# Relu-squared attention followed by a GELU MLP on one core: the same operations in a new written-out order

## The chip, the core and the metric

The kernel runs on one core of a Trainium2 chip. Its time is device microseconds per execution. Several executions were timed, and one more was taken with the hardware profiler; that one gives the trace that this document reads. An engine's name in the profile stands for: PE (TensorE, matmuls), PEld (TensorE's weight loads, which overlap PE), DVE (VectorE), ACT (ScalarE), POOL (GpSimd, which here issues the loads), SP (SyncE, which issues stores and the transposing DMAs).

## What is computed

The reference, cut to its core: attention with a squared relu in place of the softmax, over 8 batches, 12 heads, 448 rows and 64 columns a head, then an MLP of 768 to 2048 to 768 with an exact GELU over the 3584 rows that result.

```python
scores = scale * np.matmul(q, k.transpose(0, 1, 3, 2))        # q, k, v: (8, 12, 448, 64)
attn = np.maximum(scores, 0.0) ** 2 / S
attn_out = np.matmul(attn, v)                                 # heads side by side -> x (3584, 768)
h = x @ w_in                                                  # (768, 2048)
g = 0.5 * h * (1.0 + erf(h * inv_sqrt2))
out = g @ w_out                                               # (2048, 768), float32
```

## The kernel before

**The work.** A batch's attention goes by three groups of four heads. For each group and each of seven key blocks of 64, TensorE makes scores (tile `ps`, line 806, four 64-row matmuls that run side by side), ScalarE or VectorE scales them and cuts them at zero into `a_sq` (lines 823 and 825), one of the two squares them (835 on VectorE, 833 on ScalarE), and after the seventh block TensorE multiplies with `v_sb` into `pav` (line 885), which is copied out as `xT` (550, 548). The MLP's two products are made by a scheme with seven products for eight (Strassen's kind): halves of operands are added or subtracted by VectorE (`t_x`, `ws`, `s_sb`, `t_sb`), TensorE multiplies (`pe`, line 1103; `pb`, line 1256; `pso`, line 1432), and VectorE or ScalarE gathers the parts (`part`, `osb`). GELU is on ScalarE. Output rows are stored from `osb` (three buffers) by SyncE, lines 1385 and 1393.

**The operands' way.** Batches 0 and 1 are transposed on TensorE (`tp`, lines 667 and 696). From batch 2 on, q and k are loaded by GpSimd (`nq`, `nk`, lines 506 and 588) and turned by transposing DMAs that SyncE issues (line 724, `kT<-nk` and `qT<-nq`). A batch's loads wait behind small copies on GpSimd (`gate`, lines 761 and 770) until the turns of the batch before have landed, because they fill the same tile; the last batch's v load stands behind such a copy too.

**What sets the order.** Every operation is an `Op` in one list. A table, `ORDER`, names all of them one after the other, with the engine that runs each: `P` and `Q` TensorE (`Q` takes two small PSUM banks in place of a wide one), `A` ScalarE, `D` VectorE, `G` GpSimd, `S` SyncE, `Z` a matmul on zeros whose result nothing reads. The number is the operation's place in the list. So `D46` in the table says that operation 46, which either engine could do, is done by VectorE. `place()` walks the table:

```python
for word in ORDER.split():
    if word[0] == "Z":
        op, eng = next(fills), "PE"
    else:
        op, eng = self.open[int(word[1:])], names[word[0]]
        if word[0] == "Q":
            op.split()
```

Each engine then runs its own operations strictly in the table's order, and waits by semaphores for what its next operation needs. A second table, `HOMES`, gives the buffer of each tile in the wide PSUM banks (`w`, 3), the small ones (`f`, 2) and the `a_sq` and `part` buffers (`a`, 14). Times in the planner that wrote the tables are not in the kernel.

The words that the prediction speaks of: `P102`, the product with v of batch 0, group 1, second half; `P270`, a product of the first MLP block (`pe`); `P1313`, the first product with v of batch 7; `G2`, the identity matrix for the transposes; `G3`, `G6`, k of batch 0, groups 1 and 2; `G1079`, v of batch 7; `S1099`, `S1119`, `S1118`, `S1291`, `S1098`, stores; `S1266` to `S1271`, the six turns of batch 7 (even: k; odd: q; two for each group); `S1068`, `S1069`, the last two turns of batch 6.

Of the kernel before, what the change touches and what calls it, by code (L numbers as in the profile page):

```python
# [99 lines left out]
A13 A19 D16 G2 Q17 D18 P20 D21 Q14 D15 G3 P22 D23 P42 A43 P45 D46 P39 A40 G4 P32 P24 P36 A37 D33 P96  # L100
Z672 A97 D25 P54 Z1024 A55 D41 D44 D47 G6 P26 D27 G7 Q28 D29 P57 A58 G10 P30 D31 P34 D35 D38 P51 A52
P72 D73 D59 D53 P69 A70 D71 D56 Q114 P60 A61 D62 A115 G5 P48 G121 A49 P66 A67 D68 G8 P87 A88 D50 G9
D74 Q78 A79 D116 P99 A100 P84 D85 P63 Q75 A64 A65 D76 D77 A80 P105 A106 D98 P93 P108 D94 A109 D107
G11 P144 A145 P134 D135 P111 A112 P81 A82 A83 G120 D101 P132 D133 G12 P146 A147 D89 D95 D86 P167
P179 A180 P161 A162 P148 D168 A149 G124 P136 D113 P90 A91 A92 P173 D137 D110 Q164 A165 D174 P102
A103 P117 D104 A118 A119 D169 D253 P176 A177 G125 P138 D139 D175 D163 D181 P170 A171 D178 D172 P245
A246 P185 P194 A186 D187 P200 A195 D196 A201 D166 P249 A250 G123 P150 A151 P191 P197 A198 P188 D189
A192 G129 P142 D143 G122 G128 P140 D141 D190 D199 D255 P203 A204 D205 P182 A202 P215 D216 D193 P209
A210 A183 A184 P251 A252 P247 A248 D254 P221 A222 P212 A213 G127 G126 P206 A207 Q224 A225 G131 P261
P278 D257 P268 D256 D258 D260 D279 D262 D226 D259 G152 A208 G153 Q227 P218 A223 A219 D220 P285 A269  # L110
A286 P264 P281 D265 D282 P263 P280 D211 A228 D229 A217 P273 D283 P270 P287 D271 D274 D288 G243 G130
A214 Q230 D266 P290 D291 A231 A232 D376 P276 A284 P293 A294 A277 A275 P378 P395 P380 P397 D374 D375
D377 D379 P381 D383 A292 A384 A267 D396 D400 P385 P402 A403 A386 P398 A382 A399 D412 D413 D415 P416
P433 A401 A417 A434 P390 P404 D405 A406 P407 D408 P419 A289 D391 D414 P387 P436 D388 P423 P440 A272
D458 A409 A420 G240 G241 S233 P410 P393 D450 D451 A437 P425 A424 P442 D426 A441 D443 A394 A389 A411
P428 S234 Q302 D459 A303 P314 A315 G155 G156 G158 G159 A427 P445 D446 A447 P431 P448 Q308 A309 D429
D453 D454 P317 A449 A318 P418 P435 D438 D421 D460 P462 D456 A432 A392 P464 D457 A422 A439 A463 D465
A444 P320 A321 P311 A312 D319 D452 P305 P466 A467 A306 A430 D455 D310 D304 P468 D469 S236 G239 G242
S235 P329 P341 A342 S238 A330 P335 A336 A307 D461 D313 P470 D471 D316 P472 S237 P368 D494 D322 D331
A369 P362 P338 A339 G154 G157 G160 G244 G295 G296 G297 P474 D475 D337 S477 P326 D495 D496 D473 P323  # L120
A363 D364 A327 D328 D340 A324 P344 A345 D346 P332 A333 A325 P498 A499 P500 P353 D501 D334 D343 S478
A354 D355 P359 P350 A351 A360 D497 D352 P502 D503 P365 A370 A366 P347 A348 A349 P356 D357 D367 A358
A361 P504 D505 P506 S479 P532 A533 P523 D524 D507 P526 A527 P508 G298 P520 D521 D522 P514 A515 G299
G300 P371 P517 A518 P529 A530 P510 D372 D373 D588 D586 D509 D587 D534 P590 P607 A608 A591 D589 P592
D595 D516 P597 P614 A615 D598 P610 P593 D624 A611 A594 P609 D612 P602 P619 A531 P616 A613 A519 D620
D617 A618 A621 D603 P626 P643 A596 D644 P599 D600 S482 S481 A627 S483 A601 P628 P645 D528 D648 A649
D631 A632 P629 A630 P605 P622 A606 D511 D625 D525 P633 P650 D634 A623 P646 P635 S480 P547 Q538 A651
P655 A539 S476 A548 D636 A637 P638 D647 D656 A657 P641 P652 D639 A640 P544 A545 G484 G487 P541 D653
D542 A642 G301 G490 Q535 A536 P556 A557 P574 P658 A659 A575 D678 D676 D677 P680 A681 D558 P553 D537
D554 D549 D540 D679 G485 G486 G488 G489 G491 G492 P565 A566 A546 P568 A569 S661 G666 P682 D683 P684  # L130
A555 D570 D543 A685 P562 A654 A563 P577 A578 A604 S512 S660 S662 P550 D551 D552 P686 P688 P725 P571
A572 A726 P559 P716 A717 D687 D564 D696 P690 D576 D689 A718 D560 D561 D573 D579 D691 D567 P719 D720
P728 A729 S663 G669 G493 P580 A581 A582 P692 D693 P700 P722 S695 S513 S665 G672 D697 G667 G668 P734
A723 D735 D721 D701 P583 A584 A585 P731 P749 D750 P702 D703 P752 A753 P740 D741 P704 A705 P792 A732
D698 P706 D699 P708 P809 D727 D724 P794 P811 D707 D733 D788 D789 D736 P799 P816 A730 A810 D709 P712
A751 D817 P821 D814 D791 D790 D713 A793 D797 P710 A798 P795 A815 D800 D711 P812 A813 P804 D822 A796
D805 P755 A823 Q737 A756 P743 A744 P818 D826 D827 P828 P845 A846 A757 P830 P847 D819 P824 D829 P831
D833 P801 D738 A739 D850 A851 P848 A849 A834 P835 P852 A853 D802 P807 A803 A808 D832 P837 A825 P854
A745 G670 G671 D878 D836 P840 D838 S864 D855 S862 S715 D742 S664 P782 A783 Q764 A765 P857 D858 A859
S863 P843 P860 A861 D880 D766 D841 D879 P882 S714 A844 A806 A856 P933 P773 S694 P746 D747 G673 D748  # L140
A774 A934 G674 S867 G868 P884 A883 D885 D754 A839 P758 P779 D759 D760 D775 P767 D881 P886 A887 A842
A780 A768 D781 D769 P888 D889 P890 D891 A820 D898 D900 P776 A777 A778 P761 A762 P930 P770 A771 D899
D784 A763 P892 A931 D893 P894 D772 P918 A919 D895 S865 G871 G675 G874 P948 D949 G869 G870 S897 P927
A928 D929 P902 P945 D946 P960 A961 P785 A786 S866 P924 A925 A926 D947 P954 D955 P904 D903 D901 D905
P936 A937 D920 D950 P921 P906 D907 G872 G873 G875 P908 D909 P910 A787 D992 D962 D911 D990 D932 P912
D913 A938 A935 P914 S916 S896 S1066 G876 A922 A923 S1067 S1065 S1068 D915 S917 P994 A995 P942 A943
Q966 P939 D967 P957 A958 Q951 P1011 G1070 D991 D993 P997 P1001 S1064 S1069 G1073 G877 G1076 A940
G1071 G1072 G1074 D941 D956 A998 P1018 A1002 A1019 P1003 D1004 P996 P1013 A1012 D999 D1016 A1005
A968 A1000 P1023 P1006 D1007 A1008 P1014 D1015 P1030 P1047 A1048 D1024 P1020 D1028 D1021 P1032 P1049
D1052 A1017 A1031 D1035 A1022 A1036 P1033 P1050 A1051 A1034 D959 D1029 P1009 P1037 P1054 D1055 P1039  # L150
P1056 D1038 D1040 P1026 D1057 P1042 P1059 D1043 D1080 D1060 D1081 A1041 A1027 A952 P1045 P1062 A1046
A1010 A1063 P1084 A1025 D953 P984 P969 A970 A971 A1053 P978 P1086 D1085 D1082 D944 P1088 D1087 P1090
D979 D985 A1044 A1089 A1061 P972 A973 P1138 D1139 A1058 D1091 P963 A964 P1135 D1136 P975 A976 A965
D1102 A974 A977 D986 P1094 D1095 P1092 D1093 D1083 P981 P1126 D1100 D1101 G1075 A982 D983 G1077
G1078 P1144 A1145 P1104 A1127 A980 P1096 D1097 S1099 P1153 D1154 P1159 A1160 D1128 P987 D988 D989
P1123 A1124 P1150 A1151 D1140 D1155 P1106 A1105 D1107 P1129 P1120 A1121 D1122 D1152 P1132 A1130
P1108 D1109 P1198 P1196 P1213 A1133 P1215 P1110 A1214 D1103 P1112 D1218 D1111 D1197 D1113 A1131
A1161 D1201 P1114 P1116 D1192 D1193 D1134 D1195 D1115 D1117 S1119 A1125 A1137 P1162 A1163 P1141
A1142 A1143 P1168 A1169 Q1147 P1199 A1148 D1194 P1216 D1217 A1202 P1203 P1220 A1221 P1156 A1157
A1158 Q1186 D1200 P1205 P1222 D1146 D1204 D1206 P1208 D1223 A1164 A1224 P1225 P1232 P1249 A1233  # L160
A1250 D1209 A1210 P1228 A1229 D1226 D1230 D1231 P1234 P1251 D1254 A1219 D1237 P1235 P1252 D1236
A1255 D1253 A1227 A1207 P1211 A1238 A1212 D1187 D1149 P1239 P1256 A1240 A1257 P1241 P1258 D1259
D1242 P1180 A1260 D1181 Q1174 A1243 A1175 P1261 P1244 D1262 A1263 P1247 P1264 D1245 A1265 A1248
# [1607 lines left out]
```

## Time and profile before

| what | value |
|---|---|
| median of 3 runs | 359.67 us (358.12 to 360.7) |
| the profiled execution's own time | 358.11 us |
| its span, first to last instruction | 356.3 us |
| granted TensorE clock | 1.0 throughout |
| PE busy | 348.5 us, 98% |
| PEld busy | 250.1 us, 70% |
| DVE busy | 306.0 us, 86% |
| ACT busy | 262.1 us, 74% |
| POOL busy | 102.9 us, 29% |
| DMA packets | 123465, 43.01 MB |

The span is the sum that a prediction works on; 1.8 us of the execution lie around it. Busy PE counts matmuls whose ends are modelled, so it says that matmuls follow each other without a gap, not that each runs at its peak.

### The profile page before, as it was taken

To read this page: it belongs to the slowest core of one execution; us is meant where nothing else is said; L and a number is where in the kernel's file an instruction comes from. 1 tells how busy PE (TensorE), PEld (TensorE's weight loads), DVE (VectorE), ACT (ScalarE), POOL (GpSimd) and SP (SyncE) were. 2 spreads that over 40 slices of the span, in tenths; PEclk is the share of its full clock that TensorE was granted. 3 is DMA by queue.
4 is the path that set the end of the run, shared out by engine and by line. 5 is a ranking of instruction groups with operands and counts; after the bars stand their busy time and mean duration, and the time that the engine had idled before them with its cause. 6 is when DMAs were issued, how large, how long until landed. Compare 5 with 4: busy or idle time off the path is not lost.

```text
span 356.3 us, 9246 instructions
## 1 busy us (share of the span) xinstructions
PE 348.5 (98%) x3853; PEld 250.1 (70%) x3853; DVE 306.0 (86%) x524; ACT 262.1 (74%) x431; POOL 102.9 (29%) x138
## 2 busy tenths in 40 slices
PE   7799999999999999999999999999999999999995
PEld 4577789855599555896557965669669856878663
DVE  3999999999898999789996998879987998769563
ACT  4999978999968995478985689879897896126100
POOL 8565842295183101603714129001000000000000
PEclk9999999999999999999999999999999999999999
DMA  9999999999999726999899979538009001012222
GB/s 174 198 204 203 186 192 176 163 158 161 170 154 179 114 44 116 102 199 118 114 166 137 188 101 122 74 107 139 2 2 182 30 2 46 2 45 90 88 90 88
DMA packets 123465, 43.01 MB, mean 121 GB/s; under 512 B 100896, under 2 KB 120096, under 8 KB 123424
## 3 DMA queue, kind: packets, MB, share of 16 engines
q0 software_dynamic: 84432, 22.47, 66.7%
q1 hardware_dynamic: 38448, 19.50, 26.1%
q8 instruction: 30, 0.49, 0.5%
q10 hardware_dynamic: 544, 0.46, 0.4%
q14 instruction: 11, 0.09, 0.1%
HBM read 45.61 MB, written 11.01 MB: 159 GB/s over the span
## 4 chain that ended last, share of the span: by engine, by line
PE 91%; ACT 6%; DMA 1%; DVE 0%; issue 0%; DVEq 0%; ACTq 0%
PE pso L1432 36%; PE pe L1103 30%; PE ps L806 10%; PE pav L885 9%; ACT a_sq L823 5%; PE pb L1256 5%; PE psh L947 2%; DMA k<-in_k_dram 1%; ACT h_sb L1153 1%; PE tp L667 1%; ACT h_sb L957 1%; DVE nk L548 0%; PE tp L696 0%; ACT p_sb L550 0%; DVE kT L548 0%
## 5 line engine op out<-in xcount | busy, mean ns | idle before, releaser
L823 ACT ACTIVATE a_sq<-ps 128x896 bf16<-128x896 f32 (+2 forms) x145 | 117.3, 879 | 14.3 <-PE ps L806 14.1
L835 DVE TENSOR_TENSOR a_sq<-a_sq 128x896 bf16<-128x896 bf16 (+1 forms) x123 | 71.7, 612 | 1.1 <-ACT a_sq L823 0.8
L1432 PEld LDWEIGHTS <-s_sb 128*128 128x128 bf16 x456 | 42.8, 98 | 31.4 <-issue 3.7
L1103 PEld LDWEIGHTS <-win_sb 128*128 128x128 bf16 x624 | 59.3, 98 | 3.3 <-issue 1.8
L1141 DVE TENSOR_TENSOR part<-pe,part 128x448 f32<-128x448 f32 x78 | 45.6, 618 | 7.9 <-PE pe L1103 5.8
L1153 ACT ACTIVATE h_sb<-part 128x448 bf16<-128x448 f32 x78 | 43.0, 583 | 11.1 <-DVE part L1141 10.8
L806 PE MATMUL ps<-qT,kT 64*64 64x448 bf16 (+1 forms) x756 | 48.5, 337 | 2.2 <-ACT a_sq L823 1.9
L1432 PEld LDWEIGHTS <-h_sb 128*128 128x128 bf16 x336 | 31.7, 98 | 23.5 <-issue 4.9
L1103 PEld LDWEIGHTS <-ws 128*128 128x128 bf16 x468 | 44.3, 98 | 3.0 <-issue 2.7
L588 POOL DMA_DIRECT2D nk<-in_k_dram x36 | 34.8, 968 | 32.1 <-DMA kT<-nk 18.3
L833 ACT ACTIVATE a_sq<-a_sq 128x896 bf16<-128x896 bf16 x46 | 43.3, 970 | 0.3
L825 DVE TENSOR_SCALAR a_sq<-ps 128x896 bf16<-128x896 f32 (+1 forms) x40 | 39.8, 1002 | 3.3 <-PE ps L806 3.1
L1432 PE MATMUL pso<-wout_sb,h_sb 128*128 128x384 bf16 x224 | 41.1, 326 | 0.1
L1432 PE MATMUL pso<-t_sb,s_sb 128*128 128x384 bf16 x224 | 41.1, 326 | 0.0
L1432 PE MATMUL pso<-wout_sb,s_sb 128*128 128x384 bf16 (+2 forms) x232 | 41.1, 321 | 0.0
L885 PE MATMUL pav<-a_sq,v_sb 64*64 64x448 bf16 (+1 forms) x756 | 36.1, 329 | 0.2 <-DVE a_sq L825 0.2
L806 PEld LDWEIGHTS <-kT 64*64 64x64 bf16 x756 | 19.9, 105 | 21.9 <-issue 16.0
L1103 PE MATMUL pe<-t_x,win_sb 128*128 128x224 bf16 x312 | 35.3, 259 | 0.0
L550 ACT COPY part<-pe 128x448 f32<-128x448 f32 x50 | 25.0, 538 | 13.8 <-PE pe L1103 11.3
L1103 PE MATMUL pe<-xT,win_sb 128*128 128x224 bf16 x312 | 34.0, 259 | 0.0
L1103 PE MATMUL pe<-t_x,ws 128*128 128x224 bf16 x312 | 33.5, 259 | 0.0
L506 POOL DMA_DIRECT2D nq<-in_q_dram x36 | 30.1, 839 | 5.8 <-DMA wout_sb<-in_moe_w_out_dram 2.9
(72 smaller groups left out, 401.2 us busy)
## 6 DMA issues: line engine op xcount, KB each, us to landing
out_dram<-osb SPq DMA_DIRECT2D x19, 384.0 KB, 2.7
nq<-in_q_dram POOLq DMA_DIRECT2D x37, 112.0 KB, 6.3
nk<-in_k_dram POOLq DMA_DIRECT2D x36, 112.0 KB, 6.5
v_sb<-in_v_dram POOLq DMA_DIRECT2D x5, 672.0 KB, 7.9
v_sb<-in_v_dram POOLq DMA_DIRECT2D x9, 224.0 KB, 8.3
win_sb<-in_moe_w_in_dram POOLq DMA_DIRECT2D x8, 192.0 KB, 9.2
wout_sb<-in_moe_w_out_dram POOLq DMA_DIRECT2D x4, 384.0 KB, 13.5
wout_sb<-in_moe_w_out_dram POOLq DMA_DIRECT2D x1, 1536.0 KB, 18.2
```

The source lines that it names most:

```text
L506: nc.gpsimd.dma_start(nq[b][:, g0, :, e], rows)
L588: nc.gpsimd.dma_start(nk[b][:, g0, :, e], rows[:, e].rearrange("p (i d) -> p i d", d=D))
L806: nc.tensor.matmul(side(ps, e)[64 * j : 64 * j + 64, x * w : x * w + w], kT[r, g, i * 128 + 64 * j : i * 128 + 64 * j + 64], moving, start ...
L823: A.activation(to, x, AF.Relu, scale=c_att)
L825: V.tensor_scalar(to, x, c_att, 0.0, op0=mybir.AluOpType.mult, op1=mybir.AluOpType.max,)
L833: A.activation(ar, ar, AF.Square)
L835: V.tensor_mul(ar, ar, ar)
L885: nc.tensor.matmul(side(pav[0], e)[o2 : o2 + 64, :w], vt[b][r, 2 * g + e, bass.ts(i, D)], box["a2"][r, e, o : o + w], start=(i == 0), stop ...
L1103: nc.tensor.matmul(bank[name][:, y, z * HS : z * HS + HS], w[:, k, bass.ts(mm, 128)], right()[:, k], start=first and k == 0 and z == 0, st ...
L1141: V.tensor_add(get(to), ps(name), get(other))
L1153: A.activation(h_ring()[:, m : m + 2, o + half[c].start : o + half[c].stop], src().rearrange("p (x n) -> p x n", x=2), AF.Gelu,)
L1432: nc.tensor.matmul(box[bank][:, n0:n1], left()[:, kf], right()[:, kf, n0:n1], start=bool(need) and kf == 0, stop=kf == K2 - 1, skip_group_ ...
```

## The change

Only the two tables change. The list of operations, the tiles, the shapes and the count of matmuls (3853) stay. The new tables were laid out by the planner with the packets of TensorE's program counted as arriving later than before. Every line of `ORDER` and `HOMES` differs; the first two lines of `ORDER` show the kind:

```diff
-A13 A19 D16 G2 Q17 D18 P20 D21 Q14 D15 G3 P22 D23 P42 A43 P45 D46 P39 A40 G4 P32 P24 P36 A37 D33 P96
-Z672 A97 D25 P54 Z1024 A55 D41 D44 D47 G6 P26 D27 G7 Q28 D29 P57 A58 G10 P30 D31 P34 D35 D38 P51 A52
+D16 G3 G2 Q17 D18 A13 P14 D15 A19 Q20 D21 P22 D23 P45 D46 P42 A43 P39 G4 G7 P24 A40 D25 P32 D33 P36
+D37 P57 A58 Z1024 Q51 A52 Q28 D41 D29 D44 Q34 D35 D59 A47 G10 Q30 A31 P54 A55 G6 P26 D27 P99 P84 A85
```

Over the whole program ScalarE gets 427 operations instead of 416 and VectorE 507 instead of 518: 17 more squarings on ScalarE, and ten more of the relu steps on VectorE.

**GpSimd at the start.** These are GpSimd's first rows behind its constants: the identity matrix (L1554) and the loads of batch 0. Before:

```order
L1554 ISA
L1554 AFFINE_SELECT ident<-ident 128x128
L585 DMA nk<-in_k_dram 128x2x448
L501 DMA nq<-in_q_dram 112x4x256
L585 DMA nk<-in_k_dram 128x2x448
L501 DMA nq<-in_q_dram 112x4x256
L501 DMA nq<-in_q_dram 112x4x128
L608 DMA v_sb<-in_v_dram 128x2x448
```

Now:

```order
L585 DMA nk<-in_k_dram 128x2x448
L1554 ISA
L1554 AFFINE_SELECT ident<-ident 128x128
L501 DMA nq<-in_q_dram 112x4x256 x2
L501 DMA nq<-in_q_dram 112x4x128
L585 DMA nk<-in_k_dram 128x2x448
L608 DMA v_sb<-in_v_dram 128x2x448
```

The load `G3` moved ahead of the identity matrix `G2`, and the second k load, `G6`, went behind all q loads of batch 0.

**VectorE in the opening.** These are VectorE's rows from its first relu step on (L825 relu, L835 square, L548 copies out of PSUM), about the stretch from 8 to 18 us of the program before. Before:

```order
L825 TENSOR_SCALAR a_sq<-ps 128x2x224
L548 COPY qT<-tp 128x2x224 x2
L835 TENSOR_TENSOR a_sq<-a_sq 128x896 x2
L835 TENSOR_TENSOR a_sq<-a_sq 128x2x224
L548 COPY kT<-tp 128x896
L548 COPY qT<-tp 128x2x224 x3
L835 TENSOR_TENSOR a_sq<-a_sq 128x896
L825 TENSOR_SCALAR a_sq<-ps 128x896
L835 TENSOR_TENSOR a_sq<-a_sq 128x896 x6
L548 CAST xT<-pav 128x224
```

Now:

```order
L825 TENSOR_SCALAR a_sq<-ps 128x2x224
L548 COPY qT<-tp 128x2x224 x2
L825 TENSOR_SCALAR a_sq<-ps 128x896
L835 TENSOR_TENSOR a_sq<-a_sq 128x896
L548 COPY qT<-tp 128x2x224
L835 TENSOR_TENSOR a_sq<-a_sq 128x896
L548 COPY qT<-tp 128x2x224
L835 TENSOR_TENSOR a_sq<-a_sq 128x896
L548 COPY kT<-tp 128x896
L835 TENSOR_TENSOR a_sq<-a_sq 128x896 x3
L825 TENSOR_SCALAR a_sq<-ps 128x896
```

A relu step of full width now comes third, where a copy of K and the first squarings stood.

**SyncE around batch 7.** These are SyncE's rows from the last turns of batch 6 to the last turn of batch 7. Before, they are `S1069`, the stores `S1099 S1119 S1118`, `S1266`, `S1269 S1267`, the stores `S1291 S1098`, `S1268`, `S1271`, `S1270`:

```order
L724 DMA_TRANSPOSE qT<-nq 128x8x112
L1385 DMA out_dram<-osb 128x768 x3
L724 DMA_TRANSPOSE kT<-nk 128x7x128
L724 DMA_TRANSPOSE qT<-nq 128x8x112 x2
L1385 DMA out_dram<-osb 128x768 x2
L724 DMA_TRANSPOSE kT<-nk 128x7x128
L724 DMA_TRANSPOSE qT<-nq 128x8x112
L724 DMA_TRANSPOSE kT<-nk 128x7x128
```

Now they are three stores (the second is `S1099`), `S1069`, `S1068`, the store `S1098`, `S1271`, the stores `S1119 S1118`, `S1267`, `S1266`, the store `S1291`, `S1269`, `S1268 S1270`:

```order
L1385 DMA out_dram<-osb 128x768 x3
L724 DMA_TRANSPOSE qT<-nq 128x8x112
L724 DMA_TRANSPOSE kT<-nk 128x7x128
L1385 DMA out_dram<-osb 128x768
L724 DMA_TRANSPOSE qT<-nq 128x8x112
L1385 DMA out_dram<-osb 128x768 x2
L724 DMA_TRANSPOSE qT<-nq 128x8x112
L724 DMA_TRANSPOSE kT<-nk 128x7x128
L1385 DMA out_dram<-osb 128x768
L724 DMA_TRANSPOSE qT<-nq 128x8x112
L724 DMA_TRANSPOSE kT<-nk 128x7x128 x2
```

The last turns of batch 6 went behind a store that they preceded, a q turn of batch 7 (`S1271`) went ahead of two stores and of the first group's turns, and the second group's q turn (`S1269`) went behind the store `S1291`.

More of the change, by code (lines that the diff above doesn't have):

```diff
@@ L105 @@
[L105 to L114, printed above, removed]
@@ L145 @@
[L145 to L150, printed above, removed]
@@ L162 @@
-A1255 D1253 A1227 A1207 P1211 A1238 A1212 D1187 D1149 P1239 P1256 A1240 A1257 P1241 P1258 D1259
-D1242 P1180 A1260 D1181 Q1174 A1243 A1175 P1261 P1244 D1262 A1263 P1247 P1264 D1245 A1265 A1248
-D1176 Q1177 D1178 A1246 D1272 D1273 P1165 A1166 A1167 D1274 P1183 D1184 D1185 S1118 S1266 S1269
-A1170 S1267 P1298 A1299 G1480 G1079 P1276 P1278 P1295 P1171 P1292 D1182 A1277 D1279 P1280 D1281
-D1188 D1275 A1293 A1172 P1282 D1283 A1179 A1173 A1296 P1284 D1285 P1301 D1302 P1307 A1308 A1309
-P1189 P1304 A1305 P1310 A1311 P1288 D1190 D1191 D1366 P1368 D1364 D1365 D1289 S1291 D1367 P1385
@@ new lines @@
+D107 A95 G11 P144 A145 P108 A109 P81 A82 A83 G120 Q132 P134 D133 G12 P146 A147 D135 P167 A168 P161
+A162 D86 D89 D110 P179 D180 D98 D101 P148 A149 P90 A91 D92 G129 P173 A174 D169 G125 G124 Q136 D137
+Q164 A165 P102 A103 A104 D175 P117 D118 A119 P170 D171 D172 D253 P138 A139 D163 D166 D181 D254 P176
+A177 D178 P245 A246 P194 A195 P185 A186 D187 P200 G123 G128 A201 P150 A151 P249 A250 P197 D198 D199
+P188 A189 P191 A192 P142 P140 P203 A204 D141 G122 P182 D143 P209 A210 A183 D205 D193 D196 P215 A216
@@ new lines @@
+A184 P247 A248 P251 A252 P212 A213 P221 A222 G127 G126 D190 D202 P206 A207 A208 Q224 G131 P261 P278
+D257 D258 P218 A279 D255 D225 A262 A219 G152 G153 Q227 A228 P268 P285 A269 D256 P264 P281 D214 A282
+A265 P263 P280 D223 A211 D217 D259 P273 D260 P270 P287 G130 A220 D226 D229 D266 D286 D288 A289 Q230
+A231 A232 D271 P276 P293 D283 D274 A277 A294 D374 P290 D375 D377 P378 D291 P395 A396 A379 P380 P385
+P402 A275 A386 A403 A284 D376 D412 D415 P397 D400 D383 A272 P381 P398 D413 A382 P407 A399 D408 P416
@@ new lines @@
+P433 D434 A401 P404 P390 G240 G241 D450 P387 D391 A292 A384 D388 D405 A417 A392 A409 P419 P436 A437
+A389 P423 P440 A420 A441 D414 G243 D453 D457 P410 A267 D458 P393 A411 A394 S233 P425 P442 D443 S234
+Q302 A424 D426 P314 A315 A427 A303 P445 P428 P431 D429 A430 P418 D446 D451 D459 A432 Q308 A309 A444
+P317 A318 P435 D438 D421 D454 P448 A449 D456 D460 D319 P462 A463 P305 A306 P311 P320 A321 A322 P464
+A316 D465 P466 P468 D452 D304 D461 G155 G156 G158 G159 G239 A312 A467 S236 S235 P329 A406 A330 A313
@@ new lines @@
+P981 A982 P1144 A1145 P1126 A1127 D1100 D1101 D1137 D983 P1104 P1096 D1097 S1099 P1153 D1154 A977
+P1159 A1160 P987 A988 A989 P1123 D1124 P1150 A1151 P1106 D1105 P1132 A1133 P1120 A1121 P1129 D1130
+P1108 D1107 S917 D1122 D1152 D1102 D1103 D1109 D1161 A1140 A1134 A1155 P1196 P1198 P1215 P1213 A1197
+D1201 A1214 P1110 S1069 G1076 S1068 S1098 G1071 G1072 P1112 D1111 D1218 A1219 D1113 A1125 D1192
+D1193 P1114 G1074 G1075 G1077 D1115 D1131 D1194 A1128 P1116 D1117 P1162 A1163 D1146 P1141 A1142
+D1195 P1168 D1169 Q1147 A1148 A1149 A1143 P1199 P1216 D1170 G1078 S1271 D1200 P1203 P1220 Q1186
@@ new lines @@
+A1281 D1296 A1297 D1293 P1282 D1176 D1283 P1284 D1285 P1307 D1308 A1300 A1294 P1301 A1302 P1189
+D1190 A1191 P1310 P1304 D1305 A1306 A1311 D1366 P1288 D1289 S1291 D1364 D1365 D1303 P1368 P1385
+A1386 D1367 P1370 P1387 A1369 D1373 D1390 P1375 P1392 P1371 D1372 P1404 P1421 D1422 P1388 D1402
+D1309 A1376 P1377 D1378 A1393 A1312 P1380 P1397 D1381 P1286 A1389 D1398 D1403 A1379 A1382 A1405
+A1399 A1391 P1394 D1395 P1406 P1423 D1287 D1409 A1410 D1426 P1407 P1424 P1383 A1425 A1396 P1400
+A1401 P1411 A1384 P1428 A1374 A1412 S1269 G1480 S1268 Q1316 A1317 P1325 A1326 D1408 P1413 P1430
@@ new lines @@
+D1438 D1429 P1433 D1431 D1327 A1432 P1416 S1270 P1352 A1353 D1417 D1434 A1435 G1079 Q1313 A1314
+A1315 D1414 D1439 P1346 A1347 P1319 P1419 P1436 A1437 D1320 D1321 A1420 P1442 D1443 P1343 D1344
+A1427 P1340 A1341 P1328 A1329 A1418 D1440 P1444 P1334 P1322 A1323 D1335 D1445 D1336 P1358 A1359
+P1446 A1447 D1330 P1331 A1332 A1333 D1324 P1349 A1415 P1355 A1356 A1357 P1448 D1345 P1450 D1441
+D1449 D1354 P1452 D1451 D1350 D1342 D1351 D1458 D1459 P1454 D1455 S1457 A1318 P1337 D1453 S1456
+S1290 D1338 D1339 D1478 A1360 A1348 P1361 A1362 P1464 A1363 P1485 P1519 P1536 A1537 A1520 D1481
@@ L188 @@
+A1552 A1498 A1529 A1515 A1518 D1573 D1574 P1569 D1570 S1572 P1577 A1578 D1576 D1575 P1579 D1580
+P1581 D1582 P1583 P1585 D1584 D1586 D1595 D1593 P1587 D1588 S1591 D1594 P1589 D1590 S1592 P1597
+D1598 P1599 D1596 P1601 D1600 P1603 A1602 S1613 D1604 P1605 D1606 S1614 P1607 D1608 S1615 P1609
+P1610 D1612 S1617 D1611 S1616
 """
```

129 lines of the change are left out of this document (57 added, 72 removed).

## The prediction

> **What bounds the kernel now.** I read the page's shares first. They and the chain say that TensorE sets the end:
>
> ```profile
> PE 348.5 (98%) x3853; PEld 250.1 (70%) x3853; DVE 306.0 (86%) x524; ACT 262.1 (74%) x431; POOL 102.9 (29%) x138
> PE 91%; ACT 6%; DMA 1%; DVE 0%; issue 0%; DVEq 0%; ACTq 0%
> ```
>
> The change adds and removes no matmul, so it can only move TensorE's waits. The list of waits, asked for PE alone, tells how much there is to win (here its first and last row of six):
>
> ```profile
> PE ps L806 <- ACT a_sq L823: 1.9, 5, 0.7
> PE ps L806 <- DVE qT L548: 0.2, 1, 0.2
> ```
>
> Without the first idle microsecond before the spin matmuls, the other five sum to 2.9 us (1.9, 0.4, 0.2, 0.2, 0.2). All of them lie in the opening. The windows show the same: the three stretches are the opening up to P102, from there to P270, and the rest behind 90 us.
>
> ```profile
> 4.73:27.94 23.21, 20.21 (x477) 15.27 (x479) 21.80 (x42) 21.08 (x33) 15.01 (x23) 1.00 1.32 200
> 27.94:48.87 20.93, 20.88 (x341) 16.56 (x333) 20.53 (x36) 20.80 (x37) 15.49 (x20) 1.00 1.46 194
> 90.00:356.00 266.00, 262.67 (x2620) 187.15 (x2612) 223.49 (x379) 182.47 (x297) 50.33 (x66) 1.00 0.76 101
> ```
>
> The columns are PE, PEld, DVE, ACT and POOL busy, the clock, the DMA share and GB/s. In the opening VectorE is busy for 21.80 of 23.21 us, ScalarE for 21.08, TensorE for 20.21 only: there the two engines that empty PSUM lead. To 48.87 us all three are full. Behind 90 us VectorE has 42 us and ScalarE 83 us to spare, and TensorE's 3.3 us not busy lie at the tail, where nothing moves. So the place where a new order can win or lose by throughput is the first 49 us; behind it, it can lose by an operand that comes late.
>
> **Term 1, changes of tile shape.** Counted in the two orders, TensorE goes 105 times between full 128x128 products and the 64-wide ones before, 103 times now. What one costs, from the chain, where pieces are summed:
>
> ```profile
> 273.10 1.30 PE pso L1432 x8
> 129.19 1.41 PE pso L1432 x8
> 129.00 0.19 PE ps L806 x4
> 130.59 0.69 PE ps L806 x12
> ```
>
> Eight `pso` matmuls take 1.30 us among their like, 1.41 with scores behind them: 0.11. Twelve scores take 0.69 with `pso` behind them against 3 times 0.19: 0.12. Two changes fewer give **-0.2 us**.
>
> **Term 2, the opening.** The AV product P102 has the same 49 TensorE operations ahead of it in both orders. What VectorE must have finished by then differs: 41 operations before, 40 now. By kind: two relu steps more, one full square more, one K copy, one half Q copy, one `xT` copy and one half square fewer.
>
> ```profile
> L825 DVE TENSOR_SCALAR a_sq<-ps 128x896 bf16<-128x896 f32 x7 | 7.6, 1081 | 0.0
> L835 DVE TENSOR_TENSOR a_sq<-a_sq 128x896 bf16<-128x896 bf16 x33 | 19.0, 615 | 0.4 <-ACT a_sq L823 0.4
> L548 DVE COPY kT<-tp 128x896 bf16<-128x896 bf16 x5 | 3.1, 620 | 0.0
> L548 DVE COPY qT<-tp 128x448 bf16<-128x448 bf16 x6 | 2.1, 382 | 0.1
> L548 DVE CAST xT<-pav 128x224 bf16<-128x224 f32 x4 | 1.4, 382 | 0.4 <-ACT xT L550 0.4
> ```
>
> That is 2 x 1.081 + 0.615 - 0.620 - 3 x 0.382 (the half square taken as the other half sizes) = +1.0 us of VectorE ahead of P102. In the timeline of before, the last of the 41, a K copy, and P102 stand so:
>
> ```profile
> 26.97 0.62 DVE L548 COPY kT<-tp 128x896 bf16<-128x896 bf16 x1
> 27.93 0.27 PE L885 MATMUL pav<-a_sq,v_sb 64*64 64x224 bf16 x4
> 9.51 1.46 DVE L835 TENSOR_TENSOR a_sq<-a_sq 128x896 bf16<-128x896 bf16 x3 [0.44 <-ACT a_sq L823]
> ```
>
> The copy ended at 27.59, 0.34 ahead of P102. With 1.0 us more, P102 would wait 0.66; if the early relu step also fills the idle 0.44 of the third row, 0.2. So TensorE may lose 0.2 to 0.7 us here. Further on it turns: P270 has the same 86 TensorE operations ahead in both orders, and VectorE 76 before, 72 now. By kind these are two full relu steps and two squares more, one K copy, three half-size steps and four `part` copies (612 ns each) fewer: 2.16 + 1.23 - 0.62 - 1.15 - 2.45 = -0.8, or -0.5 if each of the four fewer is taken without the 0.08 by which neighbours overlap (three squares take 1.46, not 0.615 + 0.615 + 0.38). So the loss at P102 is what VectorE would otherwise have cost up to P270: a loss of 0.7 at worst, a gain of 0.5 at best, and I take **0**.
>
> **Term 3, the first loads.** `G3` no longer waits for the identity matrix:
>
> ```profile
> 0.34 0.10 POOL L1755 MEMSET const-uint8-127<- 128x1 uint8 x1
> 1.08 0.29 POOL L1554 TENSOR_SCALAR_AFFINE_SELECT ident<-ident 128x128 bf16<-128x128 bf16 x1 [0.64 <-DVE warm L1560]
> 1.42 0.85 POOL L585 DMA_DIRECT2D nk<-in_k_dram  x1
> 4.73 0.64 DVE L548 CAST nk<-k 128x512 bf16<-128x512 f32 x1 [3.72 <-DMA k<-in_k_dram]
> q10 hardware_dynamic: 318, 0.27, 79.4%
> q1 hardware_dynamic: 194, 0.09, 30.9%
> q0 software_dynamic: 2, 0.00, 1.1%
> ```
>
> The constants end at 0.44, so `G3` can be issued some 0.9 us sooner. The last three rows are the DMA queues from 3.2 to 4.2 us: the first loads of k and q fill the DMA engines (110%), and GpSimd's queue has moved two packets. The cast of k, for which VectorE and TensorE wait, starts at 4.73 when k has landed. Packets of `G3` from about 3.2 on would share with k. Nothing in the trace shows that sharing, so bounds: if k is served first, 0; if a third queue takes a third of the last 1.5 us, those take 1.5 times as long, +0.75. I take **+0.3 us**, nearer to nothing, as GpSimd's queue starts slowly. Loads that land sooner win nothing, since VectorE and ScalarE set the pace by then.
>
> [...]
>
> **Term 4, the packets of TensorE's program.** They are what the new layout counts as later. The only place where a packet and a wait of TensorE meet:
>
> ```profile
> q8 instruction: 1, 0.02, 12.2%
> 13.58 0.39 PE L806 MATMUL ps<-qT,kT 64*64 64x224 bf16 x8 [0.33 <-ACT a_sq L823]
> ```
>
> The first row is the queue of instructions from 12.5 to 13.0 us. The wait that ends at 13.58 is put down to ScalarE, whose relu step freed the bank. If the packet ended it instead, a better place for it wins 0.3 at most. I take **0**. [...]
>
> **Term 5, behind 49 us.** TensorE stands within 0.1 us of full from 28 to 90 us, so gains are nil, and I see no throughput lost: ScalarE's 11 more operations meet its 83 us of idle time. Tail order: the last product's two parts change places, but the VectorE step on it waits for both in either order: 0. Small waits that come and go I bound by the 0.7 us of the longest wait above, either way; **0**.
>
> **The sum** is -0.2 + 0 + 0.3 + 0 + 0 = +0.1 us on a span of 356.3, so 358.2 for an execution like the profiled one (358.11). The median of the runs stands 1.6 above that one, so the forecast in its terms is **359.8**. The terms' bounds, -0.2 - 0.5 - 0.3 - 0.7 = -1.7 and -0.2 + 0.7 + 0.75 + 0.7 = +2.0, give 358.0 to 361.7. A change under 1% is about what a measurement of this kernel cannot tell from none.
>
> **Rival A, all waits go** (the order finds work for each of them): 2.9 + 0.2 = -3.1 us, 356.6. For it: a re-laid order aims at just this. Against it: VectorE's 21 us ahead of P102 cannot shrink, and it gets more there. Even this is 0.9%.
>
> **Rival B, v of batch 7 comes late.** `G1079` waits for `S1269`, which now stands behind the store `S1291`. Before, gate and load had 40 us:
>
> ```profile
> 242.94 0.20 POOL L770 COPY gate<-qT 128x16 bf16<-128x16 bf16 x1 [20.75 <-DMA qT<-nq]
> 243.47 0.83 POOL L608 DMA_DIRECT2D v_sb<-in_v_dram  x1 [0.33 <-issue]
> 267.03 0.81 SPq L1385 DMA_DIRECT2D out_dram<-osb  x2
> 283.20 1.49 PE L885 MATMUL pav<-a_sq,v_sb 64*64 64x448 bf16 x28
> kT<-nk SPq DMA_TRANSPOSE x1, 3.8
> v_sb<-in_v_dram POOLq DMA_DIRECT2D x1, 672.0 KB, 6.7
> v_sb<-in_v_dram POOLq DMA_DIRECT2D x1, 672.0 KB, 9.2
> qT<-nq SPq DMA_TRANSPOSE x1, 8.6
> ```
>
> The third row is `S1291`, the fourth P1313, which stands 0.8 us earlier in the new order (fewer products ahead): needed at 282.4. The last four are landings of single issues: the turn right behind `S1291`, the fastest (the old `G1079`) and slowest v load, and the slowest turn, `S1069`. Now: 267.03 + 0.4 for the store, 3.8 for the turn, 0.5 from gate to load, 6.7 to 9.2: v is there at 278.4 to 280.9, with 1.5 to 4 us in hand. The chain of 14.9 us from turn to v is the point where it decides: a turn of 8.6 puts v at 283.2 to 285.7, up to 3.3 late, with no later work of TensorE able to pass it. Price +3.3 on the forecast's 359.8 and 0.5 of the start's upper bound: 363.6, **slower by 1.1%**. Against it: few loads run then, and the turn in that place took 3.8.
>
> **Rival C, the start and P102 both at their upper ends**: +2.0, 361.7.
>
> **Chances.** Forecast (358.6 to 361) 0.58; A and its halves (356.6 to 358.6) 0.16; C 0.15; B 0.11. Faster by over 1% needs more than all waits and a quieter chip: 0.03. Slower by over 1%: B, with 0.01 of C. The rest is within 1%. For 8 in 10 I leave out the last of A and the upper half of B, and allow for medians that scatter over 2.6 us in the runs shown: 357.4 to 362.8.
>
> **What would show it.** Term 1: `pso` and `ps` pieces of the chain as long as before. Term 2: an idle stretch of TensorE before the `pav` of P102 that VectorE ends, and none before P270. Term 3: VectorE's cast of k at 5.0 instead of 4.73. Term 4: no wait that "issue" ends near an instruction packet. Rival B: a wait of `pav` for DMA `v_sb` near 282 us. I am wrong if TensorE waits for SyncE's turns in the middle, or if the squarings that went to ScalarE hold up AV products that had no slack.

## The result, and the profile after

| | before | changed |
|---|---|---|
| median of 14 executions each | 359.78 us (358.12 to 362.75) | 357.88 us (357.45 to 358.08) |
| ratio, with its 95% interval | | 0.9942 (0.9917 to 0.9967) |
| the profiled execution | 358.11 us, span 356.3 | 357.81 us, span 356.0 |

The forecast was 359.8, no change. The median fell by 1.9 us, which is more than the measurement's uncertainty, while the two profiled executions differ by 0.3. What changed most is the scatter. Over all the sittings behind this document the old kernel ran 167 times, from 357.99 to 364.11 with a median of 358.94; 96 of these took 358.8 or more. The changed kernel ran 25 times, in two of the sittings, from 357.45 to 358.23, median 357.80. By these the gain is 1.1 us rather than 1.9. (The ratios here and below leave out executions disturbed by over 1.5%, so they aren't the quotients of the medians beside them, which are over all.)

So there are two questions: what the order does to an undisturbed execution (0.3 us), and why the old kernel's executions are late by up to some microseconds and the new one's are not.

The page of the changed kernel, its shares and its chain:

```profile
PE 348.8 (98%) x3853; PEld 249.7 (70%) x3853; DVE 305.4 (86%) x514; ACT 269.0 (76%) x442; POOL 103.3 (29%) x138
PE 93%; ACT 4%; DMA 1%; DVE 1%; issue 0%; DVEq 0%
```

The waits of PE in the changed kernel, without the one ahead of the spin matmuls:

```profile
PE ps L806 <- ACT a_sq L823: 0.6, 3, 0.2
PE tp L667 <- DVE nk L548: 0.6, 1, 0.6
PE pav L885 <- ACT a_sq L823: 0.4, 1, 0.4
PE ps L806 <- DVE xT L548: 0.3, 1, 0.3
PE psh L947 <- DMA win_sb<-in_moe_w_in_dram: 0.2, 1, 0.2
PE ps L806 <- DVE qT L548: 0.2, 1, 0.2
```

They sum to 2.3 us instead of 2.9, and all lie in the opening, as before. TensorE sets the end in both. The lists don't say where the 0.3 us came from. To see it, take places with the same TensorE work ahead in both orders: the product P102, a score block at 94 us, and the last group of products. In the timelines of PE, of the changed kernel and then of before (P102 before stands in the prediction at 27.93):

```profile
28.61 1.54 PE L885 MATMUL pav<-a_sq,v_sb 64*64 64x224 bf16 x56
94.49 0.76 PE L806 MATMUL ps<-qT,kT 64*64 64x448 bf16 x12
350.93 1.26 PE L1432 MATMUL pso<-wout_sb,s_sb 128*128 128x256 bf16 x12
```

```profile
94.10 0.76 PE L806 MATMUL ps<-qT,kT 64*64 64x448 bf16 x12
351.22 1.05 PE L1432 MATMUL pso<-wout_sb,s_sb 128*128 128x128 bf16 x12
```

The changed kernel is 0.68 us later at P102, 0.39 later at 94 us, and 0.29 earlier at the end. It loses in the opening and wins 1.0 us behind it, in bits of 0.1 to 0.2.

### The profile page after: what moved, and what is told of

It reads as the page before. It is cut to its first block, busy times and chain, and to the rows that moved or that the text cites. A ratio compares the mean times of both kernels' runs of the same rounds, so it can differ in the third digit from the quotient of the medians.

```text
span 356.0 us, 9239 instructions
## 1 busy us (share of the span) xinstructions
PE 348.8 (98%) x3853; PEld 249.7 (70%) x3853; DVE 305.4 (86%) x514; ACT 269.0 (76%) x442; POOL 103.3 (29%) x138
## 4 chain that ended last, share of the span: by engine, by line
PE 93%; ACT 4%; DMA 1%; DVE 1%; issue 0%; DVEq 0%
PE pso L1432 37%; PE pe L1103 30%; PE ps L806 10%; PE pav L885 9%; PE pb L1256 5%; ACT a_sq L823 3%; PE psh L947 2%; DMA k<-in_k_dram 1%; ACT a_sq L833 1%; PE tp L667 0%; PE tp L696 0%; ACT h_sb L957 0%; DVE kT L548 0%; DVE nk L548 0%; ACT xT L550 0%
## 5 line engine op out<-in xcount | busy, mean ns | idle before, releaser
L823 ACT ACTIVATE a_sq<-ps 128x896 bf16<-128x896 f32 (+1 forms) x135 | 108.3, 863 | 9.7 <-PE ps L806 9.6
L835 DVE TENSOR_TENSOR a_sq<-a_sq 128x896 bf16<-128x896 bf16 x106 | 61.7, 617 | 1.7 <-ACT a_sq L823 1.0
L833 ACT ACTIVATE a_sq<-a_sq 128x896 bf16<-128x896 bf16 (+1 forms) x63 | 58.2, 950 | 0.9 <-DVE a_sq L825 0.6
L825 DVE TENSOR_SCALAR a_sq<-ps 128x896 bf16<-128x896 f32 (+1 forms) x51 | 50.6, 1003 | 3.4 <-PE ps L806 2.8
L550 ACT COPY part<-pe 128x448 f32<-128x448 f32 x52 | 26.0, 539 | 14.0 <-PE pe L1103 10.1
```

Of the source, the lines that this page charges most:

```text
L823: A.activation(to, x, AF.Relu, scale=c_att)
L825: V.tensor_scalar(to, x, c_att, 0.0, op0=mybir.AluOpType.mult, op1=mybir.AluOpType.max,)
L833: A.activation(ar, ar, AF.Square)
L835: V.tensor_mul(ar, ar, ar)
```

## The experiments

### Is the scatter the kernel's own, and which engines' order carries it?

First the old kernel again, unchanged, and beside it two exchanges: the old kernel with the new order of GpSimd and SyncE, and the changed kernel with the old order of these two.

```diff
-... G2 ... G3 ... G4 ... G6 ... G7 ...   S477 S478 ... S663 S695 S513 S665 ...
+... G3 ... G2 ... G4 ... G7 ... G10 ...  S478 S476 ... S513 S663 ... S695 S665 ...   (b_GS; a_GS the other way)
```

> The kernel before, unchanged, to see what its executions do that take longer. Theory L (a load that comes late in some executions, v of batch 1 above all, which stands behind a 1.5 MB load of w_out): executions spread from 358.1 to about 362, and a longer one shows a wait of TensorE for a DMA near 50 us. Theory I (a packet of TensorE's program that comes late in some executions): the same spread, and a longer one shows an idle stretch of TensorE that no engine and no load ends, beside an instruction packet. Theory N (the spread is the chip's on that day, not the kernel's): this copy scatters less than before, or the changed kernel more, when run side by side.

> The kernel before with the changed order of GpSimd and SyncE (all loads, gates, turns and stores) and the old order of TensorE, VectorE and ScalarE. Theory L: as tight as the changed kernel, 357.5 to 358.4, median 358.0. Theory I: it scatters like before, 358.1 to 362, median 359.5 or more. Theory N: the same as whatever before does beside it.

> The changed kernel with the old order of GpSimd and SyncE, and the new order of TensorE, VectorE and ScalarE. Theory L: it scatters like before, median 359.5 or more. Theory I: as tight as the changed kernel, median 357.9, 358.1 at most. Theory N: the same as before beside it.

The copy scattered like the old kernel beside it: median 358.95 (358.14 to 360.07) against 359.01. So theory N in its first form fell: it isn't the day. Theory I fell with the profiles: in none of the longer executions below does the list of TensorE's waits name "issue". `b_GS` had 358.79 (358.33 to 359.49): less scatter, but a higher floor. Its profile shows why: TensorE waits twice for a k load, 0.6 us for G6, which the old TensorE order wants early and the new load order has behind all q loads, and 0.5 for one of batch 1 that went out at 17.90 us instead of 16.17 (list of waits of PE, `b_GS`):

```profile
PE tp L667 <- DMA nk<-in_k_dram: 1.1, 2, 0.6
```

`a_GS` took 360.66 (359.92 to 361.75), ratio 1.0045 (1.0030 to 1.0061). Turns that came too late for the new order show in the same list:

```profile
PE ps L806 <- DMA kT<-nk: 0.9, 1, 0.9
PE ps L806 <- DMA qT<-nq: 0.9, 1, 0.9
```

So an order of the queues fits its own order of the engines; whole exchanges add waits, and can't say what each half is worth. Theory L's number for `a_GS` (359.5 or more) came true, but by these added waits and not by scatter: all six of its executions are late. A third loss of `a_GS`, 0.7 us at 139 us, is the place that comes next.

The copy gave more than its time. Its profiled execution took 358.65, and as it is the same program as the one profiled at 358.11, the two can be laid beside each other instruction by instruction. Apart from small shifts that come and go, TensorE falls behind at two places only: 0.2 us at 23.3, where a load of win lands late, and 0.3 us at 140. The rows about the second, of VectorE and PE and of the stores landing, before:

```profile
137.64 0.56 DVE L1466 TENSOR_TENSOR osb<-pso,p_sb 128x384 f32<-128x384 f32 x1
139.92 0.98 PE L1432 MATMUL pso<-wout_sb,s_sb 128*128 128x384 bf16 x5
out_dram<-osb SPq DMA_DIRECT2D x1, 240.0 KB, 3.2
```

and in the slower execution:

```profile
138.22 0.56 DVE L1466 TENSOR_TENSOR osb<-pso,p_sb 128x384 f32<-128x384 f32 x1 [0.36 <-PE ps L806]
140.43 0.34 PE L1432 MATMUL pso<-wout_sb,s_sb 128*128 128x384 bf16 x1
out_dram<-osb SPq DMA_DIRECT2D x1, 240.0 KB, 3.6
```

VectorE's output step is idle 0.36 us ahead. The releaser named, a score block, is not what the step needs: before, it started at 137.64 while the like block ran (137.53 to 138.10). What it waited for is the output buffer, which the store `S695` has to leave. The store's second piece, issued at 134.30 in the one execution and 134.53 in the other, landed at 137.51, 0.13 ahead of the step, and at 138.10, 0.12 ahead of it. Behind the step VectorE has `s_sb`, and TensorE's `pso` waits for that. In the old order this step sits on the edge of a store's landing: any jitter of the store becomes time. In the new order `S513` goes out 18 us earlier (134.8 before, 116.5 now) and this step takes the buffer that `S513` frees.

### Which load or store?

One load was suspected ahead of the others, v of batch 1, which landed 1.58 us ahead of its use behind a 1.5 MB load of w_out.

```diff
-... G243 G130 ... G240 G241 ...
+... G130 ... G240 G241 G243 ...
```

> The kernel before with one move: the 1.5 MB load of w_out (G243) goes behind the v load of batch 1, group 2 (G130), and the two small w_out loads behind that, so that v has no big load ahead of it on its queue. Theory L, if that load is the one that comes late: tight, median 358.1 to 358.3. If another load is late, or by theories I and N: scatters like before, median 359.5 or more.

It scattered on: median 359.24 (358.12 to 360.79). It isn't that load. Next the store, alone, then with the turn `S664`, then with a win load as well:

```diff
-... S663 ... S695 S513 S665 ... S862 S715 S664 ...      G120 ... G12
+... S513 S663 ... S695 S665 ... S862 S664 S715 ...      G12 G120
```

> The kernel before with one store moved on SyncE's queue: S513 goes ahead of the turn S663, as in the changed kernel, so that the output buffer that op 703 (L1466, written at 137.64) takes is freed 17 us earlier, instead of by S695, whose landing at 137.51 to 138.10 is what op 703 stands behind. Theory O (stores and turns that land at the edge of their use make the spread; this one is the largest): no wait of VectorE's osb step at 137 us in the profile, the lowest execution stays at 358.1, the median falls by 0.3 to 0.5 to about 358.6, and single executions above 359.5 stay, from the other edges. Theory N (the order of TensorE, VectorE and ScalarE makes the spread): nothing changes, median 359.0, up to 360 or more.

> The same, and the turn S664 ahead of the store S715 (it landed 1.8 us ahead of its use at 160.9, behind that store; in the changed kernel 17 us ahead). Theory O: lowest 358.1, median 358.3 to 358.5, none above 359.5. Theory N: as before, median 359.0 and up to 360 or more.

> Both moves on SyncE, and on GpSimd the win load G12 ahead of the k load G120, so that the product at 23.15 us, which G12 reached 0.11 us ahead in one profile and 0.15 us late in another, has its operand some 3 us early. Theory O: 0.1 to 0.2 below the kernel with the two moves alone, median 358.2 to 358.3 and all executions within 0.8 us. Theory N: as before.

The old kernel beside them had a median of 359.14 (358.08 to 360.66). `b_S513` had 358.50 (358.17 to 359.35), ratio 0.9985 (0.9969 to 1.0002), `b_S2` 358.55 (358.21 to 359.45): the store is worth about 0.6 us in the median, the turn nothing more. That is about what theory O said, though the interval just reaches 1. Better evidence is the upper end: no execution of these two passes 359.45, while 39 of the old kernel's 167 took 359.5 or more.

`b_S2G12` was a miss: 359.62 (358.65 to 362.87). Its profiled execution took 360.87 and had lost 1.9 us by 11.5 us, ahead of the moved load's issue at 11.71, and 2.7 by 17 us. The PE rows there:

```profile
7.35 0.96 PE L667 MATMUL tp<-ident,nk 128*64 128x128 bf16 x14 [0.33 <-DMA nk<-in_k_dram]
8.24 1.15 PE L806 MATMUL ps<-qT,kT 64*64 64x224 bf16 x20
```

A load of k is late, and the scores take 1.15 us where the old kernel's took 0.67; the next part is on this. What the win load's place does by itself stays open.

The opposite, putting the two places of SyncE's queue back in the changed kernel:

```diff
-... S513 S663 ... S695 ...  S665 S664 ... S715 ...
+... S663 ... S695 S513 ...  S665 S715 S664 ...
```

> The changed kernel with these two places of SyncE's queue put back: the store S513 behind S695, the turn S664 behind the store S715. Theory O: it scatters again, lowest 357.5, median 358.2 to 358.8, some above 359. Theory N: as tight as the changed kernel, 357.5 to 358.1, median 357.9.

It took 358.57 (358.42 to 359.23), against 357.45 to 358.23 for the changed kernel as it is (in other sittings). Every execution is slower, by about 0.8 us in the median. The new order has this output step 0.9 us earlier than the old one, so with the old store order it always waits. VectorE's rows in the changed kernel, and with the two places put back:

```profile
136.76 0.55 DVE L1466 TENSOR_TENSOR osb<-pso,p_sb 128x384 f32<-128x384 f32 x1
```

```profile
138.08 0.56 DVE L1466 TENSOR_TENSOR osb<-pso,p_sb 128x384 f32<-128x384 f32 x1 [0.97 <-DMA out_dram<-osb]
139.69 0.38 PE L806 MATMUL ps<-qT,kT 64*64 64x448 bf16 x4 [0.31 <-DVE a_sq L825]
```

Here the wait has its own name, the store, and the one of TensorE behind it too. SyncE's rows show the cause: two issues of the store S513 at 116.54 in the changed kernel, and all four together at 134.38 with the places put back:

```profile
116.54 1.55 SPq L1393 DMA_DIRECT2D out_dram<-osb  x2
134.12 0.78 SPq L1393 DMA_DIRECT2D out_dram<-osb  x2
```

```profile
134.38 1.84 SPq L1393 DMA_DIRECT2D out_dram<-osb  x4
```

So this part of the gain is shown from both sides. Laid beside the changed kernel's, the profile also says what it is worth: of the 1.0 us by which TensorE ends later in it, the store makes 0.5, at 139 us; 0.25 are there by 25 us, ahead of both places; and 0.23 come at 166.8 us, where a q turn that went out at 164.74 instead of 160.43 landed only 0.14 ahead of the scores that use it. In `a_GS`, with the old queue order too, the same step of VectorE waits 1.18 us for the store.

### The step of one microsecond that is left

The times of `b_S513` and `b_S2` fall into two groups: 16 of 24 from 358.17 to 358.81, and 8 from 359.06 to 359.45. The profile of `b_S2` was taken of an execution of 359.11. Its PE rows, and those of before, from the first scores on:

```profile
7.74 1.15 PE L806 MATMUL ps<-qT,kT 64*64 64x224 bf16 x20
8.81 0.96 PE L696 MATMUL tp<-ident,nq 112*64 112x112 bf16 x16
```

```profile
7.32 0.67 PE L806 MATMUL ps<-qT,kT 64*64 64x224 bf16 x20 [0.17 <-DVE qT L548]
7.92 0.58 PE L696 MATMUL tp<-ident,nq 112*64 112x112 bf16 x16
```

The same matmuls take 1.15 and 0.96 us instead of 0.67 and 0.58. TensorE ran at half rate here up to about 10.4 us, before up to about 6.4; 1.0 us of this was still missing at the end. The profile's clock column says 1.00 in both, so it is the rows that tell. Nine spin matmuls (on zeros, ahead of the work) stand at the start. They are 512 columns wide and start 0.427 us apart; a `pso` matmul of 384 columns starts every 0.163 us later on, which in proportion makes 0.217 for 512, so the spin runs at half rate. To see whether the work ahead of the first transposes bears on the step, I changed their number:

```diff
-SPIN = 9
+SPIN = 10      (b_spin10, a_spin10)
+SPIN = 7       (b_spin7, a_spin7)
```

> The kernel before with ten spin matmuls in place of nine (0.447 us each at the half rate): TensorE stays busy to 5.43 us, so the idle 0.41 before the first transposes is gone. [...] Theory O alone (stores and turns at the edge make all the spread): the same as before, median 359.0, 4 in 10 or more above 359.

> The kernel before with seven spin matmuls: TensorE is idle from 4.12 to 5.42 us. [...] Theory O alone: the same as before, since nothing waits for a spin matmul: median 359.0, lowest 358.1.

> The changed kernel with seven spin matmuls, to learn what the half rate costs it. Theory W1 (the changed order keeps TensorE busy enough to be at full rate early in every execution, but would pay like before): median 358.8 to 359.5, lowest 357.5. Theory W2 (the changed order hides a late full rate, as it is bound by VectorE and ScalarE there): median 357.9 to 358.2. Theory O alone: 357.9, unchanged.

> The changed kernel with ten spin matmuls; a candidate for the fastest. Theory W1 and O: unchanged, 357.5 to 358.1, median 357.9, as it had no late execution. Theory W2: lower by up to 0.2, where a late full rate was not hidden wholly, median 357.7.

With seven, the old kernel's median was 359.11 (358.08 to 361.90), 11 of 12 at 358.7 or more, against 358.70 (357.99 to 362.23) beside it; the ratio, 1.0012 (0.9995 to 1.0030), is not clear of none. With seven, the changed kernel's was 358.84 (357.81 to 359.12). In the profiles with seven TensorE is idle for 1.27 us ahead of the first transposes in the old kernel (0.41 with nine) and at half rate up to about 8.7 us (6.4); in the changed one idle for 1.41 (0.55) and at half rate up to about 9.5 (5.6 at most). So the half rate costs the changed order the same 1.0 us (358.84 against 357.80 with nine): W1 holds as to the price, and W2 falls. That the changed order is at full rate early in every execution, as W1 also says, this run can't show. The changed kernel's first scores with seven:

```profile
7.57 1.15 PE L806 MATMUL ps<-qT,kT 64*64 64x224 bf16 x20
```

With ten, the changed kernel stayed at 357.87 (357.52 to 358.10). The old kernel with ten was no faster: median 359.30 (358.17 to 360.55) against 358.70. Its profiled execution took 360.55 at full rate by 7.7 us and shows other causes, of which the win load at 24.68 us cost 0.4 and two cost more. In the list of waits of PE, and the landings of k's second load and of the turn `S479`, of before and of this run:

```profile
nk<-in_k_dram POOLq DMA_DIRECT2D x1, 224.0 KB, 4.9
qT<-nq SPq DMA_TRANSPOSE x1, 6.2
```

```profile
PE ps L806 <- DMA qT<-nq: 0.9, 1, 0.9
PE tp L667 <- DMA nk<-in_k_dram: 0.8, 1, 0.8
nk<-in_k_dram POOLq DMA_DIRECT2D x1, 224.0 KB, 6.2
qT<-nq SPq DMA_TRANSPOSE x1, 9.1
96.52 0.76 PE L806 MATMUL ps<-qT,kT 64*64 64x448 bf16 x12 [0.91 <-DMA qT<-nq]
```

The load took 6.2 us instead of 4.9 with the same issue time (1.42), and the turn 9.1 instead of 6.2. In the old order this turn lands 1.4 us ahead of its use at 94.10; in the changed one 2.3 ahead, and a turn 2.9 late would still show there, by 0.6.

### Late first loads

To learn what late first loads cost, four more identity matrices were made on GpSimd at the start; and in another run the identity went ahead of G3 again; and the changed kernel ran once more as it is.

```diff
+    for _ in range(4):
+        make_ident()
     ctx.enter_context(tc.manual_schedule())     (b_late, a_late)
-D16 G3 G2 Q17
+D16 G2 G3 Q17                                   (a_G2)
```

> The kernel before with the identity matrix made five times instead of once on GpSimd, which puts its loads of the opening some 1.1 us later in every execution, as they were by themselves in one that took 360.55 (G3 landed at 7.63 there instead of 6.27). Theory R (the old order pays for late first loads, the changed order hides them): median 359.3 to 359.8. Theory F (full rate and S695 alone make the spread): 359.0, unchanged.

> The changed kernel with four identity matrices made ahead of G3, so that its loads are 1.0 us later. Theory R: median 357.9 to 358.2. Rival R2 (the changed order pays as much, but its loads are never late): median 358.7 to 359.2.

> The changed kernel with the identity matrix G2 ahead of the load G3 again, as before the change. By the prediction's third term: the cast of k 0.2 to 0.3 earlier, span 0.2 shorter, median 357.6. By what the profiles show since (k lands at 4.58 to 4.98 in both orders): unchanged, 357.9. Theory R2, if the place of G3 keeps its loads in time: it scatters, median 358.5.

> The changed kernel, unchanged, for more of its executions. If the half rate of TensorE can last to 10.5 us here as it did in the old kernel in about 3 of 10: 3 or 4 of 12 at 358.6 to 359.1. If not: all within 357.4 to 358.2.

Beside an old kernel of 358.61, `b_late` took 360.36 (359.79 to 362.85), ratio 1.0064 (1.0036 to 1.0093), and `a_late` 360.06 (358.37 to 361.59). Theory R falls: the changed order hides late loads no better, and the price is above what R2 said too. The pair is not exact. In `a_late` G3 still went out at 1.25, ahead of the added work, and the q loads and what follows them came 1.5 us later, which its waits show; and the profiled execution of `b_late` was still at half rate at 10.9 us, that of `a_late` at full rate by 5.3. A wait of `a_late`:

```profile
PE tp L696 <- DMA nq<-in_q_dram: 1.1, 2, 0.9
```

`a_G2` had 357.88, ten of eleven within 357.74 to 358.08 and one at 361.12. `a_copy` had 357.70 (357.45 to 358.23), ratio 0.9968 (0.9945 to 0.9991): again no late execution.

Last, the first two differences of the orders, each by itself in the old kernel with `S513` moved:

```diff
-D16 G2 Q17 D18 P20 D21 Q14 D15 G3
+D16 G3 G2 Q17 D18 P20 D21 Q14 D15               (b_S513_G3)
+D16 G2 Q17 D18 Q14 D15 P20 D21 G3               (b_S513_Q14)
```

> The kernel before with the store S513 ahead of the turn S663 and the load G3 ahead of the identity G2. If the place of G3 decides on the late executions of the opening: none of 12 in the step at 359.1 to 359.5, all within 358.1 to 358.8. If not: 3 to 5 of 12 there, as with S513 alone, and the median at 358.5.

> The kernel before with S513 ahead of S663 and the first q transposes (Q14 and their copy) ahead of the second k transposes (P20), as in the changed kernel, and nothing else. If the order of TensorE's first transposes decides on the late full rate: none of 12 in the step at 359.1 to 359.5. If not: 3 to 5 of 12 there, median 358.5.

`b_S513_G3`: median 358.16 (357.78 to 359.11) beside 359.16, ratio 0.9978 (0.9964 to 0.9992), eight at 357.78 to 358.27 and four at 358.94 to 359.11. The step is still there, so the place of G3 doesn't decide it. Two moved words win a good part of the gain; the place of G3 was not tried in the old kernel without the store. `b_S513_Q14`: 358.70 (357.90 to 361.91), with four above 360. It is no cure either, and why it scatters I can't say.

**What stays open.** The three old-order kernels `b_S513`, `b_S2` and `b_S513_G3` have the step in 12 of 36 executions, the changed kernel in 0 of 25, though half rate and late loads would cost it as much. The 36 and the 25 come from different sittings; but `a_undo`, in one sitting with 24 of the 36, has no such step either, as its 12 lie within 0.8 us. The traces with nine spin matmuls agree: three of ten with TensorE's old order have the half rate past 10 us (`b_S2`, `b_S2G12`, `b_late`), the others up to 6.9 at most; the six with the changed order have it up to 6.5 at most. That it comes less often there is measured; what in the new order brings this about is not. And of the step itself only one execution, that of 359.11, was seen from inside.

No kernel tried was faster than the changed one beyond its scatter.

## Why the prediction was wrong, by its steps

**The step that failed** is the sentence "The median of the runs stands 1.6 above that one, so the forecast in its terms is 359.8". It took the 1.6 us as a constant that any order would carry, and thought of a smaller one only as "a quieter chip". But the changed kernel's median stands 0.07 above its profiled execution, so most of the 1.6 belongs to the old order. As far as the runs show, it is made of three things: about 0.6 us in the median by a buffer step 0.13 us behind a store's landing; single late executions by late loads and by a turn with 1.4 us in hand; and a step of 1.0 us by an opening that is late in some executions, for a reason that stays open. The forecast for an execution like the profiled one, 358.2, stands 0.4 from the 357.81 measured; that it stands so near is partly luck, as the parts below were off both ways. The forecast for the median stands 1.9 away. And a change under 1% is not "what a measurement of this kernel cannot tell from none": the interval here, 0.33% to 0.83%, is clear of none.

**The waits I counted were those of one lucky execution.** Its list of waits had nothing behind 49 us, so term 5 said that "gains are nil" there. Store S695 is the counterexample: no wait in the profile, about 0.6 us in the median (359.14 to 358.50), and 0.5 in the profile when it was put back.

**Term 1** (-0.2): the pieces cost what they did, in the changed kernel's chain:

```profile
263.98 1.41 PE pso L1432 x8
272.86 1.30 PE pso L1432 x8
```

But the stretch behind P102 won 1.0 us, not 0.2. Take the time from the first score of a block to the first `pso` behind it, less 0.189 us for every four scores: these changes cost 31 times 146 ns before, 30 times 129 now, which is 0.65 less in all, and the second profiles of each kernel say the same (147 and 129). Three of them cost 0.27 to 0.33 in the old order without a wait that the list shows. I had priced all alike from one at 0.12. This is read from the traces, not tried by a run.

**Term 2** (0, between -0.5 and +0.7): P102 came 0.68 later, the upper bound, and 0.30 later in the trace of `a_copy`. Its `pav` had no wait of its own by VectorE, which was the sign to look for; the delay had come in ahead of it. The 188 score matmuls ahead of P102 took 8.4 us from start to start besides their listed waits, 7.1 before. What held them is not shown, so that VectorE's added work did it is not shown either. The half that surely failed is the turn: at P270 the changed kernel was still 0.61 behind (49.48 against 48.87).

**Term 3** (+0.3): the cast of k and G3's issue in the changed kernel:

```profile
4.92 0.59 DVE L548 CAST nk<-k 128x512 bf16<-128x512 f32 x1 [3.90 <-DMA k<-in_k_dram]
1.25 0.85 POOL L585 DMA_DIRECT2D nk<-in_k_dram  x1 [0.80 <-POOLq L1755]
```

The cast moved from 4.73 to 4.92, which looks like what the term told, but it is scatter: in the second profiles it started at 4.95 in the old kernel (`b_copy`) and at 4.37 in the changed one (`a_copy`). G3 went out only 0.17 earlier, not 0.9, as GpSimd sat idle for 0.80 us behind its constants, which the term had not reckoned with. And `a_G2`, which takes the swap back, had 357.88, not less than the 357.70 of `a_copy` beside it. So the runs show nothing of the +0.3, and none shows how the queues share the DMA engines: the bound of 0.75 was an estimate.

**Term 4** (0) held in the profile: no wait that "issue" ended, and nothing tells of a packet of instructions.

**Rival B** held in its working and did not happen. The gate, the v load, its landing and P1313:

```profile
270.59 0.83 POOL L608 DMA_DIRECT2D v_sb<-in_v_dram  x1 [0.33 <-PE pe L1103]
v_sb<-in_v_dram POOLq DMA_DIRECT2D x1, 672.0 KB, 9.1
282.39 1.49 PE L885 MATMUL pav<-a_sq,v_sb 64*64 64x448 bf16 x28
```

v landed at 279.7, 2.7 us in hand, where 1.5 to 4 was forecast. (The "chain of 14.9 us" in it is the time that there was; by its own rows the chain takes 11.0 to 13.5.) **Rival A** had the right sign for the wrong reason: the waits of the opening fell by 0.6 us only, and 3.1 was not to be had.

## What to carry to other kernels

Look at the list of times before the profile: if the executions scatter by more than the edit is worth, the scatter is part of the time, and the profiled execution may be one that shows none of it. Then ask of each buffer, load and turn how far its landing lies ahead of its use, not only which wait is listed; whatever has less in hand than a landing scatters by (here 0.13 us against a store's 0.4) is a cost to come. Two profiles of the same program, laid beside each other instruction by instruction, name such places better than any single page.

## What the runs showed of the hardware

**TensorE's start.** The moment at which TensorE leaves the half rate varies between executions: about 6.4 us before and 10.4 in `b_S2`, whose program is the same up to 110 us; still to come at 10.9 in `b_late`, where a matmul on zeros took 0.63 us instead of the 0.38 in `a_late`; at most 5.6 in the changed kernel's profile. The clock column said 1.00 throughout. Between the two executions of before and `b_S2` the moment differs by 4.0 us and the end by 1.0 us, which is 0.3% of the span and as much as the whole question here. With two spin matmuls fewer it came later, but in `b_late` TensorE was idle for only 0.37 us ahead of the first transposes, and it came later still; what sets the moment isn't shown.

**Landings.** The same transfer took 3.2 us before and 3.6 in the copy (store), 4.9 before and 6.2 in `b_spin10` (k load), 6.2 and 9.1 in the same two (turn), with the issue at the same place in the program.

**A wait that names the wrong engine.** The step at 138.22 is put down to a score block on TensorE, though the buffer's store was what it waited for; only in `a_undo` and `a_GS`, where the wait was 0.97 and 1.18, did the same step name the DMA.
